# Planner with measured durations and a measured transfer rate, in the two mixed stretches of a long-convolution and MLP kernel

## The chip, the cores and the metric

The kernel runs on one core of one Trainium2 chip. The metric is the device time of one execution in microseconds; of several runs the median counts. One execution of the kernel was also recorded by the hardware profiler, and all rows below come from that one.

## What is computed

Two batches of 12480 positions with 128 channels. A filter is made from position embeddings by a small MLP and an exponential window, the product x * v is convolved with it along the sequence (by FFT in the reference), the result is multiplied by x, and every position then goes through a leaky MLP of width 2048.

```python
h_mlp = np.maximum(pos_emb @ w1, 0.0) @ w2
h_filt = h_mlp * np.exp(-0.01 * pos)[:, None]
u = x * v
Uf, Hf = np.fft.rfft(u, n=2 * S, axis=1), np.fft.rfft(h_filt, n=2 * S, axis=0)
y = np.fft.irfft(Uf * Hf[None], n=2 * S, axis=1)[:, :S, :]
attn = x * y
h = attn.reshape(B * S, D) @ w_in
out = (np.maximum(h, 0.0) + alpha * np.minimum(h, 0.0)) @ w_out
```

## The kernel before

The FFT is done as matmuls, on values split into two float16 halves (a high part and the remainder). The 128 channels come in two groups. For each group the kernel takes chunks of four channels through a first transform over time (stage 1), then runs a loop over pairs of frequencies that multiplies with the filter (stage 2), then transforms back (stage 3) and stores to g_d in HBM. Behind that comes the MLP (phase B), which holds most of the span and is not touched.

Stage 1 of one pair of chunks is, per chunk: a load of x and of v (lines 696, 697), the product P = x * v (line 700), its square on ACT (703); per pair the norm by PE (711) and the sum and the scale of the pair on DVE (717, 332 to 334, the last writes s_u); per chunk again the scaling S (728), the high half on ACT (734), the remainder L (737), twelve matmuls on PE (771 to 773), and the split of their result into z by ACT (783) and DVE (786). P, S and L may run on DVE or on POOL. There are 16 pairs in each group.

The first mixed stretch interleaves stage 1 of the first group with the making of the filter: sixteen hidden-layer products (load 401, PE 406, DVE 409, ACT 413), their sum (DVE 426, "gather"), the scales, eight parts (ACT 451, DVE 452), the w2p halves (444, 445) and the filter's final products (PE 467 to 469, ACT 488, DVE 492). The second mixed stretch lies between the two frequency loops. It interleaves the end of the first loop, stage 3 of the first group (PE 986 to 988, ACT 998 and 1000, DVE 1003, store 1019) and stage 1 of the second group, whose filter chunks are loaded again (758). The loads of the next loop's tables (817) close it.

In both, the order on each engine's queue comes from a planner, the class Plan. Each operation is entered with an engine, a duration in ns, what it reads and writes, and buffers it needs from small pools (in the second stretch: three PSUM tiles "mm", seven x, three v, three uhl, two gst). Plan.run then lists operations: it takes the engine on which something can start first, lets all that could start there within `patience` ns of it compete, and takes the one with the smallest start plus `urge` times its due place. The due place is a + b * i for the i-th step of its kind, from `pace` (h: hidden layer in the first stretch, filter chunks in the second; w: rest of the filter; u, v: pairs of chunks; s: stage 3). An operation that may go to DVE or POOL takes the engine on which it would end first, with `bias` ns added to DVE. Only the resulting order, engine and buffer are used: at run time each engine works through its queue in that order, and waits by semaphores.

```python
near = [c for c in could[best[1]] if c[0] <= best[0][0] + self.patience]
t, _, k = min(near, key=lambda c: c[0] + self.urge * c[1])
```

All loads and stores go out through the SP queue in the planned order, so an issue that waits for a buffer holds those behind it. The rows name the tiles "ring" and "first" (the buffers of both pools), "mm" and "mb" (PSUM), "z" and "s_u".

## Time and profile before

| | us |
|---|---|
| median of three timed runs | 1669.67 |
| lowest and highest of them | 1668.25, 1672.24 |
| the profiled execution | 1673.31 |
| its span | 1671.4 |
| DVE, ACT, POOL busy in the span | 1305.9, 1335.6, 1055.1 |
| PE busy (modelled ends) | 1565.8 |

The mixed stretches can be told from the timeline of DVE: the first runs from the start to about 149 us, the first frequency loop to about 264, the second mixed stretch to about 393, and the second loop starts at 399. In a group of instructions, "x27 | 36.2, 1346 | 13.5" means 27 instructions, 36.2 us busy, 1346 ns each on average, and 13.5 us in which the engine sat idle just before one of them; what ended the idle time follows. A wait "A <- B" says that A, first in its queue, waited for B.

### The profile page before, as it was taken

The page shows a single profiled execution, that of the slowest core. Times are in us where ns is not written, and L with a number is a line of the kernel's source. Part 1 is how long each engine was busy: PE and PEld are TensorE (multiplying, and loading weights), DVE is VectorE, ACT ScalarE, POOL GpSimd, SP SyncE. Part 2 cuts the span into 40 slices and gives each one's busy share as a digit, 9 for nine tenths or more (in the row PEclk, how much of TensorE's full clock was granted, in tenths as well). Part 3 has the DMA queues.
Part 4 walks back from the last instruction along what each step waited for, and adds up shares of the span by engine and source line. Part 5 has one row for each costly group of instructions (what it writes and reads, how often), then busy time and mean ns, then how long its engine had stood idle before and what let it go on. Part 6 is the DMA issues. An engine that isn't in the chain of part 4 may idle for free.

```text
span 1671.4 us, 34331 instructions
## 1 busy us (share of the span) xinstructions
PE 1565.8 (94%) x13452; PEld 1105.8 (66%) x13452; DVE 1305.9 (78%) x1892; ACT 1335.6 (80%) x2211; POOL 1055.1 (63%) x742
## 2 busy tenths in 40 slices
PE   6878887998998699999999999999999999999998
PEld 4778777888998456666666666566666666666664
DVE  7888999887998577777777777777777777777775
ACT  5776776776876588888888888888888888888886
POOL 6586887886987455665556655565556655565554
PEclk8897998999999899999999999999999999999999
DMA  7443345874447902022020220212202112022000
GB/s 207 123 134 131 112 136 167 241 231 142 135 135 207 232 26 56 20 74 56 20 56 20 75 55 20 56 35 59 55 21 55 54 41 56 20 63 62 25 11 20
DMA packets 95567, 143.95 MB, mean 86 GB/s; under 512 B 7121, under 2 KB 64179, under 8 KB 93965
## 3 DMA queue, kind: packets, MB, share of 16 engines
q1 hardware_dynamic: 94285, 141.06, 29.6%
q8 instruction: 105, 1.72, 0.5%
q10 hardware_dynamic: 1120, 0.70, 0.1%
q14 instruction: 57, 0.47, 0.1%
HBM read 100.06 MB, written 41.68 MB: 85 GB/s over the span
## 4 chain that ended last, share of the span: by engine, by line
PE 74%; DVE 10%; POOL 4%; issue 4%; DMA 4%; ACT 3%; SPq 0%; POOLq 0%; ACTq 0%; DVEq 0%
PE hp L1244 30%; PE o L1244 30%; DVE ring L885 4%; DMA first<-in_xv 2%; POOL ring L737 2%; DVE ring L895 2%; PE yp L279 1%; PE yp L280 1%; PE yp L281 1%; PE mm L986 1%; PE mm L988 1%; PE mm L987 1%; POOL ring L700 1%; DVE z L786 1%; POOL ring L728 1%
## 5 line engine op out<-in xcount | busy, mean ns | idle before, releaser
L1244 PEld LDWEIGHTS <-w 128*128 128x128 f16 x6144 | 591.7, 97 | 431.6 <-issue 15.2
L1331 POOL TENSOR_TENSOR g_lo<-ring,g_hi 128x780 f16<-128x780 f32 x288 | 479.7, 1670 | 483.4 <-ACT g_hi L1330 483.4
L1324 DVE SCALAR_TENSOR_TENSOR ring<-ring,keep,hp 128x780 f32<-128x780 f32 x512 | 524.8, 1025 | 270.5 <-ACT ring L1323 261.4
L1323 ACT ACTIVATE ring<-hp 128x780 f32<-128x780 f32 x512 | 419.1, 818 | 162.3 <-PE hp L1244 161.4
L1244 PE MATMUL hp<-ah,w 128*128 128x390 f16 x2048 | 506.3, 328 | 3.7 <-DVE ring L1324 2.7
L1244 PE MATMUL o<-g_hi,w 128*128 128x390 f16 x2048 | 504.3, 328 | 0.9 <-ACT ot L1345 0.7
L1330 ACT ACTIVATE g_hi<-ring 128x780 f16<-128x780 f32 x512 | 433.5, 847 | 0.4 <-DVE ring L1324 0.3
L1244 PE MATMUL hp<-alo,w 128*128 128x390 f16 x1024 | 253.3, 328 | 0.8 <-DVE alo L1236 0.8
L1244 PE MATMUL o<-g_lo,w 128*128 128x390 f16 x1024 | 252.7, 328 | 0.6 <-POOL g_lo L1331 0.6
L1331 DVE TENSOR_TENSOR g_lo<-ring,g_hi 128x780 f16<-128x780 f32 x224 | 229.1, 1023 | 0.0
L1206 POOL TENSOR_TENSOR gl<-gt,gh 90x1024 f16<-90x1024 f32 x62 | 154.5, 2491 | 1.5 <-ACT gh L1205 1.5
L885 DVE TENSOR_TENSOR ring<-mm,ring 128x512 f32<-128x512 f32 (+2 forms) x188 | 116.2, 658 | 11.3 <-ACT ring L873 8.7
L986 PE MATMUL mm<-t,z 128*128 128x128 f16 x512 | 104.5, 235 | 10.5 <-DVE ring L1003 5.6
L912 POOL TENSOR_TENSOR z<-ring,z 128x512 f16<-128x512 f32 x88 | 105.0, 1194 | 6.8 <-ACT z L908 6.8
L987 PE MATMUL mm<-t,z 128*128 128x128 f16 x512 | 103.7, 234 | 0.0
L988 PE MATMUL mm<-t,z 128*128 128x128 f16 x512 | 103.6, 234 | 0.0
L771 PE MATMUL mm<-t,ring 98*128 98x180 f16 x320 | 83.5, 264 | 18.7 <-DVE z L786 5.2
L890 POOL TENSOR_TENSOR ring<-ring 128x256 f32<-128x256 f32 (+1 forms) x90 | 81.2, 902 | 30.7 <-DVE ring L885 22.2
L783 ACT ACTIVATE z<-mm 128x720 f16<-128x720 f32 (+1 forms) x99 | 73.9, 759 | 32.0 <-PE mm L773 31.6
L786 DVE TENSOR_TENSOR z<-mm,z 128x720 f16<-128x720 f32 (+1 forms) x99 | 85.2, 876 | 17.5 <-ACT z L783 16.8
L1003 DVE TENSOR_TENSOR ring<-mm,ring 90x504 f32<-90x504 f32 (+2 forms) x132 | 80.4, 655 | 13.9 <-ACT ring L1000 12.6
L773 PE MATMUL mm<-t,ring 98*128 98x180 f16 x320 | 83.6, 264 | 7.4 <-POOL ring L737 7.3
(195 smaller groups left out, 2955.3 us busy)
## 6 DMA issues: line engine op xcount, KB each, us to landing
g_d<-ring SPq DMA_DIRECT2D x32, 720.0 KB
gt<-g_d SPq DMA_DIRECT2D x16, 1440.0 KB
ring<-in_tw SPq DMA_DIRECT2D x34, 512.0 KB
ring<-in_xv SPq DMA_DIRECT2D x72, 196.0 KB
xt<-in_xt SPq DMA_DIRECT2D x31, 390.0 KB
out_t<-ot SPq DMA_DIRECT2D x31, 390.0 KB
first<-in_xv SPq DMA_DIRECT2D x56, 196.0 KB
first<-in_tw SPq DMA_DIRECT2D x12, 512.0 KB
```

Source lines behind the costliest of these rows:

```text
L786: ve.tensor_tensor(out=zb[:, 1, :, x:y, cs], in0=pv()[:, :, x:y], in1=zb[:, 0, :, x:y, cs], op=ALU.subtract)
L885: ve.tensor_tensor(out=t[:, :, m], in0=p[:, :, m], in1=hs[:, a:a + 1, m].to_broadcast([128, 2, (b1 - b0) * 2 * ZC]), op=ALU.mult)
L912: e.tensor_tensor(out=zl, in0=v, in1=zh, op=ALU.subtract)
L986: te.matmul(o, hi, t3[:, 0], start=True, stop=False)
L987: te.matmul(o, hi, t3[:, 1], start=False, stop=False)
L988: te.matmul(o, lo, t3[:, 0], start=False, stop=True)
L1206: po.tensor_tensor(out=dl, in0=src, in1=dh, op=ALU.subtract)
L1244: te.matmul(o[:, b, :TOK], w, d[:, b], start=start and n == 0, stop=stop and n == 2)
L1323: ac.activation(neg, h, AF.Relu, scale=-1.0)
L1324: ve.scalar_tensor_tensor(out=acts[n], in0=neg, scalar=keep[:, f:f + 1], in1=h, op0=ALU.mult, op1=ALU.add)
L1330: ac.activation(gh, a, AF.Copy)
L1331: (po if n % 2 or n % NFT == 0 else ve).tensor_tensor(out=gl, in0=a, in1=gh, op=ALU.subtract)
```

## The change

Only the planner's numbers change. The constructor gets a factor `flow`, 1 by default, that multiplies the duration of every DMA entry; both mixed stretches set it to 360 / 255, so a transfer is planned at 255 bytes per ns instead of 360. Durations of P, S and L and of the filter's part are replaced. The due places, `urge`, `patience` and `bias` of both stretches are replaced. The last plan, before phase B, keeps its numbers.

```diff
+        self.guard, self.bias, self.warm, self.flow = {}, 0, 0, 1
...
     def op(self, engine, ns, fn, r=(), w=(), rows=128):
         k = len(self.ops)
+        ns = ns * self.flow if engine == "DMA" else ns
...
-            P.op("DVE", dve_ns(2 * w), lambda: ve.scalar_tensor_tensor(out=lo, in0=src, scalar=sr, in1=hi, op0=ALU.mult, op1=ALU.subtract),
+            P.op("DVE", 1080, lambda: ve.scalar_tensor_tensor(out=lo, in0=src, scalar=sr, in1=hi, op0=ALU.mult, op1=ALU.subtract),
...
-                    P.op({"DVE": dve_ns(512), "POOL": 1225}, 0, product, r=[v[j]], w=[x[j]])
+                    P.op({"DVE": 880, "POOL": 1320}, 0, product, r=[v[j]], w=[x[j]])
...
-                    P.op({"DVE": 600, "POOL": 1001}, 0, scaled, r=[("s", g, n)], w=[x[j]])
+                    P.op({"DVE": 1150, "POOL": 1060}, 0, scaled, r=[("s", g, n)], w=[x[j]])
...
-                    P.op({"DVE": 600, "POOL": 1113}, 0, low, r=[x[j]], w=[h])
+                    P.op({"DVE": 1000, "POOL": 1260}, 0, low, r=[x[j]], w=[h])
...
+            P.flow = 360 / 255
...
-            P.pace.update(h=(0, 692), w=(18681, 2576), u=(10132, 13596), v=(98023, 3578))
-            P.urge, P.patience, P.bias = .5, 100, 1112
+            P.pace.update(h=(-48954, 2278), w=(20007, 3535), u=(21788, 17237), v=(94626, 3276))
+            P.urge, P.patience, P.bias = 3.7, 44, 1354
...
+            P.flow = 360 / 255
...
-            P.pace.update(h=(-9e3, 100), s=(0, 3600), u=(20394, 3768))
-            P.urge, P.patience, P.bias = 3, 50, 1377
+            P.pace.update(h=(-30228, 41505), s=(-14272, 7297), u=(23122, 6183))
+            P.urge, P.patience, P.bias = 3.1, 0, 911
```

The changed file has one more line from line 143 on, two more from 1051 and three more from 1070, so line 409 of before is 410 of after, 700 is 701, 1003 is 1004 and 1019 is 1020.

Near the start of the first stretch, on DVE, before: hidden rows (409) mixed with the first pair's sum and scale (717, 332 to 334) and a product (700).

```order
L409 SCALAR_TENSOR_TENSOR z<-mm_95,ring 128x336
L717 TENSOR_REDUCE mb_97<-mb_97 128x8
L332 TENSOR_SCALAR mb_97<-mb_97 128x8
L333 TENSOR_SCALAR mb_97<-mb_97 128x8
L334 TENSOR_SCALAR s_u<-mb_97 128x8
L409 SCALAR_TENSOR_TENSOR z<-mm_96,ring 128x336
L409 SCALAR_TENSOR_TENSOR z<-mm_94,ring 128x336
L700 TENSOR_TENSOR ring<-ring,first 98x512
L409 SCALAR_TENSOR_TENSOR z<-mm_95,ring 128x336
L409 SCALAR_TENSOR_TENSOR z<-mm_96,ring 128x336
L409 SCALAR_TENSOR_TENSOR z<-mm_94,ring 128x336
L700 TENSOR_TENSOR ring<-ring,first 98x512
```

The same place in the changed kernel, where the first pair's scale follows the last hidden row and stands right ahead of the gather (427):

```order
L410 SCALAR_TENSOR_TENSOR z<-mm_94,ring 128x336
L410 SCALAR_TENSOR_TENSOR z<-mm_95,ring 128x336
L410 SCALAR_TENSOR_TENSOR z<-mm_96,ring 128x336
L410 SCALAR_TENSOR_TENSOR z<-mm_94,ring 128x336
L718 TENSOR_REDUCE mb_97<-mb_97 128x8
L333 TENSOR_SCALAR mb_97<-mb_97 128x8
L334 TENSOR_SCALAR mb_97<-mb_97 128x8
L335 TENSOR_SCALAR s_u<-mb_97 128x8
L427 TENSOR_REDUCE n_113<-nq 128x1
L428 TENSOR_SCALAR nb<-ones,n_113 128x128
L333 TENSOR_SCALAR mb_98<-n_113 128x1
```

All sixteen hidden rows now stand ahead of any work on x and v. The second pair's sum and scale stood ahead of the gather too (rows 717, 332 to 334 again, a few rows on); in the changed kernel they stand behind seven of the eight parts (453) and twelve filter halves (493).

Near the start of the second stretch, on DVE, before: pairs of stage-3 rows (1003) ahead of the first scale, which row 334 writes.

```order
L700 TENSOR_TENSOR ring<-ring,first 98x512
L912 TENSOR_TENSOR z<-ring,z 128x2x3x64
L1003 TENSOR_TENSOR ring<-mm_96,ring 90x2x63x4 x2
L1003 TENSOR_TENSOR ring<-mm_94,ring 90x2x63x4 x2
L1003 TENSOR_TENSOR ring<-mm_95,ring 90x2x63x4 x2
L717 TENSOR_REDUCE mb_97<-mb_97 128x8
L1003 TENSOR_TENSOR ring<-mm_96,ring 90x2x63x4 x2
L786 TENSOR_TENSOR z<-mm_94,z 128x180x4
L332 TENSOR_SCALAR mb_97<-mb_97 128x8
L333 TENSOR_SCALAR mb_97<-mb_97 128x8
L334 TENSOR_SCALAR s_u<-mb_97 128x8
```

The same place in the changed kernel, where four rows less of stage 3 (1004, "x2" counts two) stand ahead of that scale and an S (729) follows it at once:

```order
L913 TENSOR_TENSOR z<-ring,z 128x2x3x64
L1004 TENSOR_TENSOR ring<-mm_96,ring 90x2x63x4 x2
L1004 TENSOR_TENSOR ring<-mm_94,ring 90x2x63x4 x2
L1004 TENSOR_TENSOR ring<-mm_95,ring 90x2x63x4 x2
L787 TENSOR_TENSOR z<-mm_96,z 128x180x4
L718 TENSOR_REDUCE mb_97<-mb_97 128x8
L333 TENSOR_SCALAR mb_97<-mb_97 128x8
L334 TENSOR_SCALAR mb_97<-mb_97 128x8
L335 TENSOR_SCALAR s_u<-mb_97 128x8
L729 TENSOR_TENSOR ring<-ring,s_u 98x512
```

With those just ahead of the pieces (four before, two after), twelve rows of stage 3 precede the first scale before, and eight now. Before, a run of four S rows (728) on DVE comes a little later; the changed kernel has none.

At the end of the second stretch, on SP, before: the last store of stage 3 (1019), then three filter chunks (758) and the next loop's tables (817).

```order
L696 DMA ring<-in_xv 98x512
L697 DMA first<-in_xv 98x512
L758 DMA ring<-h_d 98x1024
L1019 DMA g_d<-ring 90x16x128
L758 DMA ring<-h_d 98x1024 x3
L817 DMA first<-in_tw 128x2048
L817 DMA ring<-in_tw 128x2048 x3
```

The same place in the changed kernel:

```order
L1020 DMA g_d<-ring 90x16x128
L759 DMA ring<-h_d 98x1024
L1020 DMA g_d<-ring 90x16x128
L759 DMA ring<-h_d 98x1024
L818 DMA first<-in_tw 128x2048
L818 DMA ring<-in_tw 128x2048
L1020 DMA g_d<-ring 90x16x128
L818 DMA ring<-in_tw 128x2048 x2
```

The last stores now alternate with the filter chunks, and the very last one stands behind two table loads.

Counted over each stretch, the engines of P, S and L move as follows.

| | DVE before: P, S, L | DVE after | POOL before | POOL after |
|---|---|---|---|---|
| first stretch | 8, 9, 2 | 13, 4, 1 | 24, 23, 30 | 19, 28, 31 |
| second stretch | 5, 9, 0 | 11, 5, 1 | 27, 23, 32 | 21, 27, 31 |

## Rows read from the trace of the kernel before

**Rows 1.** Busy time by stretch; the first row names the columns:

```profile
core 0: us, PE busy (x) PEld busy (x) DVE busy (x) ACT busy (x) POOL busy (x), PEclk, DMA share, GB/s
0.00:149.00 149.00, 110.96 (x1315) 98.50 (x1316) 118.50 (x198) 102.64 (x184) 100.95 (x85) 0.85 0.51 152
264.00:393.20 129.20, 112.04 (x1444) 106.07 (x1443) 108.87 (x197) 90.68 (x210) 102.20 (x86) 0.92 0.72 209
344.00:393.20 49.20, 43.38 (x518) 40.72 (x517) 39.03 (x70) 36.61 (x78) 42.27 (x37) 0.90 0.67 197
```

**Rows 2.** Instruction groups, 0 to 152 us: count, busy, mean, idle:

```profile
L786 DVE TENSOR_TENSOR z<-mm,z 128x720 f16<-128x720 f32 x47 | 41.1, 898 | 8.8 <-ACT z L783 8.4
L737 POOL TENSOR_TENSOR ring<-ring 98x512 f16<-98x512 f32 x30 | 38.2, 1287 | 13.7 <-ACT ring L734 13.6
...
L700 POOL TENSOR_TENSOR ring<-ring,first 98x512 f32<-98x512 f32 x20 | 27.4, 1377 | 17.9 <-DMA first<-in_xv 16.5 <-PE mm L773 1.3
L728 POOL TENSOR_TENSOR ring<-ring,s_u 98x512 f32<-98x512 f32 x23 | 25.4, 1120 | 7.8 <-DVE s_u L334 4.0 <-DVE mb L332 3.8
...
L492 DVE TENSOR_TENSOR z<-mm,z 84x512 f16<-84x512 f32 x16 | 10.1, 676 | 0.8 <-ACT z L488 0.7
...
L452 DVE SCALAR_TENSOR_TENSOR z<-z,sr 128x672 f16<-128x672 f32 x8 | 9.2, 1171 | 0.0
...
L445 DVE SCALAR_TENSOR_TENSOR w2p<-w2b,w2p 128x256 f16<-128x256 f32 x4 | 3.6, 947 | 0.0
```

**Rows 3.** Timeline of DVE, 0 to 60 us: start, length, instruction:

```profile
7.34 0.51 DVE L409 SCALAR_TENSOR_TENSOR z<-mm,ring 128x336 f32<-128x336 f32 x1 [1.31 <-PE mm L406]
8.46 0.51 DVE L409 SCALAR_TENSOR_TENSOR z<-mm,ring 128x336 f32<-128x336 f32 x1 [0.61 <-PE mm L406]
...
26.75 0.17 DVE L334 TENSOR_SCALAR s_u<-mb 128x8 int32<-128x8 int32 x1
...
29.93 0.17 DVE L426 TENSOR_REDUCE n<-nq 128x1 f32<-128x16 f32 x1 [0.64 <-ACT mm L413]
```

**Rows 4.** Timeline of POOL, 0 to 152 us, two rows:

```profile
51.37 3.38 POOL L737 TENSOR_TENSOR ring<-ring 98x512 f16<-98x512 f32 x2 [10.16 <-ACT ring L734]
...
144.06 1.15 POOL L737 TENSOR_TENSOR ring<-ring 98x512 f16<-98x512 f32 x1 [0.25 <-ACT ring L734]
```

**Rows 5.** Instruction groups, 255 to 398 us:

```profile
L737 POOL TENSOR_TENSOR ring<-ring 98x512 f16<-98x512 f32 x32 | 41.4, 1306 | 2.1 <-ACT ring L734 2.1
...
L1003 DVE TENSOR_TENSOR ring<-mm,ring 90x504 f32<-90x504 f32 x64 | 40.4, 671 | 9.0 <-ACT ring L1000 8.4
...
L700 POOL TENSOR_TENSOR ring<-ring,first 98x512 f32<-98x512 f32 x27 | 36.2, 1346 | 13.5 <-DMA first<-in_xv 13.1
...
L728 POOL TENSOR_TENSOR ring<-ring,s_u 98x512 f32<-98x512 f32 x23 | 24.1, 1061 | 8.4 <-DVE s_u L334 8.4
...
L728 DVE TENSOR_TENSOR ring<-ring,s_u 98x512 f32<-98x512 f32 x9 | 11.0, 1249 | 0.0
...
L700 DVE TENSOR_TENSOR ring<-ring,first 98x512 f32<-98x512 f32 x5 | 4.9, 976 | 1.0 <-DMA first<-in_xv 1.0
```

**Rows 6.** Timeline of POOL, 252 to 320 us, two rows:

```profile
284.95 2.04 POOL L728 TENSOR_TENSOR ring<-ring,s_u 98x512 f32<-98x512 f32 x2 [6.55 <-DVE s_u L334]
286.94 5.87 POOL L737 TENSOR_TENSOR ring<-ring 98x512 f16<-98x512 f32 x4
```

**Rows 7.** Line 728, 255 to 400 us: min/median/max ns:

```profile
L728 DVE TENSOR_TENSOR ring<-ring,s_u x9: 678/1336/1667, 287.3 to 379.5; 98x512 f32<-98x512 f32 x9
```

**Rows 8.** Waits, 255 to 395 us: total us, times, longest us:

```profile
POOL ring L700 <- DMA first<-in_xv: 13.1, 9, 2.3
...
SPq L696 <- POOL ring L737: 35.0, 19, 5.3
```

**Rows 9.** Chain of waits, 255 to 400 us: shares by line, and one piece:

```profile
by line: POOL ring L737 16.4%; DMA first<-in_xv 15.0%; issue 14.1%; POOL ring L728 7.0%; POOL ring L700 5.4%; DVE ring L1003 3.3%; DVE ring L728 3.3%; DVE ring L885 3.2%; DMA g_d<-ring 3.1%; DVE z L786 3.1%; DVE ring L895 3.0%; PE mm L773 2
...
275.78 4.55 DMA g_d<-ring
```

More of the change, by code (lines that the diff above doesn't have):

```diff
@@ L135, in __init__ @@
         self.size, self.fifo, self.loose = dict(pools), {p: [] for p in pools}, set()
-        self.guard, self.bias, self.warm = {}, 0, 0
+        self.guard, self.bias, self.warm, self.flow = {}, 0, 0, 1
     def buf(self, pool):
```

## Prediction

> **What bounds the kernel now.** I read first the busy time by stretch. The change reorders two stretches only: from the start to 149 us, and from 264 to 393 us; behind the second, every engine's rows stand as before, apart from line numbers. In neither stretch is one engine full: in the first DVE works 118.5 of 149 us and POOL 101.0; in the second PE 112.0 of 129.2 (modelled ends), DVE 108.9, POOL 102.2 [rows 1]. So what counts is how order and waits couple them.
>
> Next the chain of waits of the second stretch. Lines 737, 728 and 700 on POOL hold 28.8% of it and the loads of v ("first<-in_xv") 15.0%; the largest DVE line has 3.3% [rows 9]. It is a ring: the loader waits for POOL's line 737 to give an x buffer back (35.0 us, 19 times), POOL's line 700 waits for the load (13.1 us, 9 times) [rows 8]. Over the last 49.2 us POOL is busy for 42.3 [rows 1].
>
> In the first stretch, read the timelines. DVE reaches the filter's sum (line 426, "gather") at 29.93 us, and has written the second pair's scale at 26.75 + 0.17 = 26.9 [rows 3]. POOL then sits for 10.16 us before its line 737 at 51.37, because ACT's order holds that row's input behind filter work, and runs its last line 737 until 144.06 + 1.15 = 145.2 [rows 4].
>
> **The change part by part.** Four edits give the planner longer DVE prices, slower transfers, new urgencies and new limits. No instruction's work changes; engine and place do. I write P, S and L for line 700's product, 728's scaling and 737's subtraction (701, 729, 738 after).
>
> *Second stretch, engine choice.* Counted in the order, POOL had 27 P, 23 S, 32 L and gets 21, 27, 31. At 1.346, 1.061 and 1.306 us [rows 5] that is 36.3 + 24.4 + 41.8 = 102.5 before and 28.3 + 28.6 + 40.5 = 97.4 after: about -5.1 by means, -4.3 against the 101.7 that the three groups really add to. I take -4.3. DVE had 5 P, 9 S and gets 11 P, 5 S, 1 L: 6 x 0.976 - 4 x 1.249 [rows 5] + one L, for which I take POOL's 1.306, is +2.2 us, inside the 129.2 - 108.9 = 20.3 us that DVE idles [rows 1]. But the two engines slow each other: four L on POOL took 5.87 us [rows 6], 1.47 each, where one alone took 1.15 [rows 4], while DVE ran S rows. That is +0.3 us on POOL per such DVE row, and there are 3 more: +0.9. Net -3.4. It lies on the path, since POOL and its loads lead the chain.
>
> The same S takes DVE from 678 to 1667 ns [rows 7]. The Trainium skill (SBUF — State Buffer, "Who interferes with whom") says why: a DVE instruction with two SBUF inputs and a GpSimd one that reads SBUF shut each other out for the whole instruction. By that rule each of the 3 added DVE rows would cost POOL a full 0.68 us, 2.0 in all, and the net would be -2.3 instead of -3.4. The mean of the four L, +0.3, speaks for less.
>
> *Second stretch, start.* POOL idles 6.55 us up to 284.95 for the first scale [rows 6]. Ahead of that scale DVE now has 8 rows of line 1003 (1004 after) instead of 12: 4 x 0.671 = 2.7 us sooner [rows 5]. POOL and its loads are 44% of the chain [rows 9], so I book half, -1.4; bounds 0 and -2.7.
>
> *Second stretch, end.* Stage 3 now lasts to the end: 5 z rows instead of 12 follow its last pair on DVE. POOL's last S S L L stays last, so this is booked at 0. The last g_d store goes out behind two table loads, and the next loop's second product waits for it. A store takes 4.55 us [rows 9], with four z pieces and the unscale rows ahead of that product as cover. If the loads are late, it costs up to 4.5; if the evened-out tail shortens PE's queue, up to -3.
>
> *First stretch.* DVE now takes all 16 hidden rows (410) before any work on u. In before, two P, two z rows, one S and two scales stood between them. Hidden rows come every 1.12 us at best (7.34 to 8.46, the second and third); before, the sixteen and the gather took from 7.34 to 29.93, 1.5 us each [rows 3]. With 14 more from 7.34, at 1.12 or at 1.5 us and 0.51 for the last, they end at 23.5 or 28.9; I take the gather at 26.5, 3.4 sooner. The price is at the second pair's scale. Between gather and it stand now 7 parts (1.171), 12 halves of the filter (0.676), 4 w2p rows (0.947) and 2 z rows (0.898) [rows 2]: 8.2 + 8.1 + 3.8 + 1.8 = 21.9 us, and about 4 us of small rows, an estimate (a dozen at 0.17 [rows 3], and the norms of w2b). So it comes at 26.5 + 26 = 52.5, say 53 us, where it was 26.9.
>
> POOL's three groups sum to the same 97.5 us in both orders (24 P, 23 S, 30 L before; 19, 28, 31 after, at 1.377, 1.120, 1.287 [rows 2]). By 53 us it can have done 10 P, 2 S, 2 L, 18.6 us; 78.9 are left, so it ends at 132 plus its idle time. Before, at 51.37, it had done 10 P, 4 S, 4 L, 23.4 us; 74.1 were left and took until 145.2, with 19.7 idle. Break-even is 145.2 - 132 = 13.3 us of idle. With 19.7 the stretch is +6.4 longer; with half, 10, it is -3. I take 13, a change of 0: six P now stand in a row on POOL while it waits, so five pairs lie ready for the scales, and much of the old idle time followed from x buffers held through the 10.16 us. DVE's count barely moves (8 P, 9 S, 2 L to 13, 4, 1), 5 x 0.976 - 5 x 1.249 and one L less, some 2.7 us less by the prices above. Range -6 (7 us of idle) to +9 (rival A).
>
> **Sum.** -3.4 - 1.4 + 0 + 0 = -4.8 us. The profiled execution took 1673.3 us (span 1671.4), so it would give 1668.5. That execution is 3.6 us above the median of the three timed runs, 1669.67, so I predict 1669.67 - 4.8 = 1664.9.
>
> **The rivals.** A difference of 0.2%, 3.3 us, is about what a measurement of this kernel can tell from no change; below 1666.3 is faster, above 1673.0 slower.
>
> *A, POOL's backlog in the first stretch decides (slower).* If hidden rows still come every 1.5 us, the gather falls near 29.5, the second scale near 55.5, and POOL with the old 19.7 us of idle ends at 55.5 + 78.9 + 19.7 = 154.1, +8.9. With -4.8 from the second stretch: 1673.8. It decides once POOL's last L there ends later than 153.3 (+8.1 - 4.8 = +3.3). For it: 19.7 idle us was normal. Against: half of that was waiting for loads and for ACT.
>
> *B, the ring of x buffers holds the second stretch (same).* POOL's saved time turns into waiting for loads, since seven x buffers and a load remain in the ring; only the earlier start counts, -1.4: 1668.3. For it: 13.1 us of load waits already [rows 8]; DMA is 72% busy [rows 1]. Against: over the last 49 us POOL is busier than the transfers (86% to 67% [rows 1]).
>
> *C, the new prices fix the coupling in both stretches (much faster).* POOL idles only 7 us after the second scale, -6, and the second stretch gives its bounds, -4.3 - 2.7 = -7.0: 1656.7. For it: the old plan priced S at 600 ns on DVE, and its mean was 1249 [rows 5]. Against: a mean of 678 to 1667 is not a duration.
>
> *D, the change does not do what it says:* the prices hold only for the old overlap and are wrong again in the new order. Then nothing systematic is left, and it lands with B.
>
> **How the numbers follow.** Forecast 0.37, C 0.17, B with D 0.24, A 0.22. The forecast's own range is 1660 to 1666.3, so faster is 0.37 + 0.17 = 0.54, same 0.24, slower 0.22. For the range I add the ends of the first stretch to the bounds of the second: -6 - 7 = -13, and a little for a shorter tail, gives 1655; +9 with -4.8, and part of the store's 4.5, gives 1677. About one case in ten lies beyond each end: 1655 to 1677.
>
> **What would show it.** In the profile after: the gather by 27 us, and the second scale near 53; POOL's last L of the first stretch at 142 to 148; no wait as long as 10 us on POOL before line 738; the first S of the second stretch some 3 us sooner after its first P; POOL's three groups there near 98 us in sum; the span from the second stretch's first P to its last L shorter by about 5 us. I am wrong if the first stretch ends after 153 us, if POOL's load waits in the second rise from 13.1 by what its work falls, or if the loop behind it opens with DVE waiting for a store.

## The result, and the profile after

The changed kernel takes 1654.61 us (median of 4 runs, 1650.64 to 1657.97), the kernel before 1668.96 us (4 runs beside them): a ratio of 0.9911, with a 95% interval of 0.9883 to 0.9938. That is 14.4 us less, where 4.8 were forecast; the time lies just below the low end of the range, 1655. The two profiled executions stand further apart: 1673.31 us before and 1655.36 after (spans 1671.4 and 1653.6).

The two traces give the gain to the two mixed stretches, in nearly equal halves. Below, the first product of loop 1 (line 886; 885 before) marks the end of the first stretch, and the same line's first row in loop 2 marks the end of the second, which starts with its first P on POOL. P, S and L are the product, the scaling and the subtraction as in the prediction.

| | before | after | |
|---|---|---|---|
| first stretch, from the start | 151.9 us | 143.4 | -8.5 |
| loop 1, to the first P | 112.4 | 112.7 | +0.3 |
| second stretch, first P to loop 2 | 134.7 | 126.9 | -7.8 |
| from there to the end | 1272.4 | 1270.6 | -1.8 |

Both stretches gained more than the range had allowed them (6 and 7 us). One trace tells a stretch's time only to about 3 us: the first two experiments below have stretches in which DVE, ACT and POOL run the same rows in the same order as here, and there the order of the kernel before took 153.4 us in the first stretch (151.9 here), and that of the changed kernel 124.0 in the second (126.9 here). Smaller differences between two traces are not read as differences.

**First stretch.** DVE's timeline after (columns: start, us, engine, line, operation, tiles, count, idle time before and its releaser): the second and the last of the sixteen hidden rows, and the gather, at 29.93 before [rows 3]; then two pieces of POOL's, the first S of the second pair, and POOL's last L (144.06 before [rows 4]).

```profile
7.16 0.51 DVE L410 SCALAR_TENSOR_TENSOR z<-mm,ring 128x336 f32<-128x336 f32 x1 [1.13 <-PE mm L407]
...
21.09 0.51 DVE L410 SCALAR_TENSOR_TENSOR z<-mm,ring 128x336 f32<-128x336 f32 x1 [0.88 <-PE mm L407]
...
22.37 0.16 DVE L427 TENSOR_REDUCE n<-nq 128x1 f32<-128x16 f32 x1
...
51.41 2.64 POOL L729 TENSOR_TENSOR ring<-ring,s_u 98x512 f32<-98x512 f32 x2 [11.26 <-DVE s_u L335]
...
137.12 1.16 POOL L738 TENSOR_TENSOR ring<-ring 98x512 f16<-98x512 f32 x1 [1.51 <-ACT ring L735]
```

POOL waits 11.26 us for the second pair's scale, as was foreseen (it comes at 51.4; the prediction said 53). But then it runs almost through: 86.9 us from there to the end of its last L, against 93.8 before. The windows view of those stretches, before and then after (columns: busy time and count of PE, weight loads, DVE, ACT and POOL, then granted clock, DMA share, GB/s):

```profile
51.40:145.20 93.80, 73.02 (x1025) 70.41 (x1022) 76.89 (x127) 68.20 (x108) 71.91 (x59) 0.84 0.48 144
51.40:138.30 86.90, 70.73 (x984) 66.22 (x981) 76.43 (x131) 68.47 (x110) 78.16 (x64) 0.90 0.54 165
```

78.16 of 86.9 us busy leaves 8.7 idle, where it was 21.9 before (the prediction's 19.7 counts the work by means, 74.1 us, where 71.9 were run). What POOL waited for from 51.5 us on (columns: line waited for, us, times, longest), after, then before; the longest one of each is the wait that ends at 51.4:

```profile
POOL ring L729 <- DVE s_u L335: 13.8, 4, 11.3
POOL ring L738 <- ACT ring L735: 4.2, 3, 1.7
POOL ring L701 <- DMA ring<-in_xv: 1.0, 2, 0.7
POOL ring L701 <- DMA first<-in_xv: 0.7, 2, 0.4
```

```profile
POOL ring L737 <- ACT ring L734: 12.8, 3, 10.2
POOL ring L700 <- DMA first<-in_xv: 6.7, 5, 3.1
POOL ring L728 <- DVE mb L332: 3.8, 1, 3.8
POOL ring L700 <- issue: 3.1, 1, 3.1
POOL ring L728 <- DVE s_u L334: 3.0, 3, 2.4
POOL ring L700 <- PE mm L773: 1.3, 1, 1.3
POOL ring L700 <- DMA ring<-in_xv: 1.1, 1, 1.1
```

Waits for x and v behind the scale fell from 7.8 us (6.7 + 1.1) to 1.7. That is 6.1 of the 13.2 us of idle time that went; waits for scales, without the one that ends at 51.4, gave another 4.3 (6.8 to 2.5), and the other waits the rest. Ahead of the scale the load waits stayed: over the whole stretch POOL waits 14.6 us for v, against 16.5 before.

**Second stretch.** The windows view, cut at the first S (first P to first S, then first S to the last L), before and then after:

```profile
264.30:284.90 20.60, 16.16 (x218) 15.66 (x216) 17.89 (x31) 12.29 (x36) 9.25 (x9) 0.83 0.61 174
284.90:392.70 107.80, 95.11 (x1218) 89.64 (x1218) 90.68 (x166) 77.89 (x174) 92.44 (x76) 0.94 0.74 215
```

```profile
256.10:270.90 14.80, 12.56 (x164) 12.37 (x165) 13.28 (x25) 8.74 (x26) 8.46 (x8) 0.77 0.44 132
270.90:372.70 101.80, 91.76 (x1246) 87.36 (x1245) 92.73 (x171) 80.56 (x180) 89.38 (x74) 0.98 0.78 225
```

The end of the stretch after, in the timelines of POOL (its last two L) and DVE:

```profile
370.38 2.32 POOL L738 TENSOR_TENSOR ring<-ring 98x512 f16<-98x512 f32 x2
...
374.82 1.27 DVE L1004 TENSOR_TENSOR ring<-mm,ring 90x504 f32<-90x504 f32 x2 [0.41 <-ACT ring L1001]
...
378.23 0.97 DVE L787 TENSOR_TENSOR z<-mm,z 128x64 f16<-128x64 f32 x2 [0.45 <-ACT z L784]
...
382.97 1.29 DVE L886 TENSOR_TENSOR ring<-mm,ring 128x512 f32<-128x512 f32 x2 [1.20 <-ACT ring L874]
```

So the 7.8 us are made of four pieces: the first S comes 5.8 us sooner after the first P (20.6 to 14.8); from there to the last L POOL works 3.1 us less (92.4 to 89.4) and idles 3.0 us less (15.4 to 12.4); and 4.0 us are given back behind the last L, since loop 2 now starts 10.3 us after it (372.7 to 383.0), where it was 6.3: DVE still has stage-3 rows and z rows until 379.2. POOL's three groups and its waits for loads, to be held against [rows 5] and [rows 8]:

```profile
L738 POOL TENSOR_TENSOR ring<-ring 98x512 f16<-98x512 f32 x31 | 38.6, 1260 | 4.8 <-ACT ring L735 4.8
L729 POOL TENSOR_TENSOR ring<-ring,s_u 98x512 f32<-98x512 f32 x27 | 31.7, 1190 | 8.3 <-DVE s_u L335 8.3
L701 POOL TENSOR_TENSOR ring<-ring,first 98x512 f32<-98x512 f32 x21 | 27.2, 1305 | 3.4 <-DVE ring L1004 2.1 <-DMA first<-in_xv 1.4
L701 DVE TENSOR_TENSOR ring<-ring,first 98x512 f32<-98x512 f32 x11 | 13.2, 1210 | 2.4 <-POOL ring L738 2.4
L729 DVE TENSOR_TENSOR ring<-ring,s_u 98x512 f32<-98x512 f32 x5 | 4.1, 829 | 0.1
```

### The profile page after: what moved, and what is told of

It is laid out like the page before. It is cut to its first block, busy times and chain, and to the rows that moved or that the text cites. A ratio compares the mean times of both kernels' runs of the same rounds, so it can differ in the third digit from the quotient of the medians.

```text
span 1653.6 us, 34337 instructions
## 1 busy us (share of the span) xinstructions
PE 1558.2 (94%) x13452; PEld 1097.7 (66%) x13452; DVE 1305.6 (79%) x1894; ACT 1335.1 (81%) x2211; POOL 1052.9 (64%) x740
## 4 chain that ended last, share of the span: by engine, by line
PE 76%; DVE 9%; POOL 5%; DMA 4%; issue 3%; ACT 3%; SPq 1%; POOLq 0%; ACTq 0%; DVEq 0%
PE o L1247 31%; PE hp L1247 31%; DVE ring L886 4%; DVE ring L896 2%; POOL ring L738 2%; DMA first<-in_xv 1%; PE yp L280 1%; PE yp L281 1%; PE yp L282 1%; PE mm L987 1%; POOL ring L729 1%; PE mm L989 1%; PE mm L988 1%; PE mm L861 1%; PE mm L859 1%
## 5 line engine op out<-in xcount | busy, mean ns | idle before, releaser
L886 DVE TENSOR_TENSOR ring<-mm,ring 128x512 f32<-128x512 f32 (+2 forms) x188 | 116.2, 658 | 12.1 <-ACT ring L874 11.3
L987 PE MATMUL mm<-t,z 128*128 128x128 f16 x512 | 104.2, 234 | 14.6 <-ACT z L909 7.3
L891 POOL TENSOR_TENSOR ring<-ring 128x256 f32<-128x256 f32 (+1 forms) x90 | 81.3, 903 | 32.6 <-DVE ring L886 26.5
L787 DVE TENSOR_TENSOR z<-mm,z 128x720 f16<-128x720 f32 (+1 forms) x99 | 85.3, 875 | 5.7 <-ACT z L784 5.4
L772 PE MATMUL mm<-t,ring 98*128 98x180 f16 x320 | 80.2, 254 | 10.0 <-DVE ring L493 3.1
L987 PEld LDWEIGHTS <-z 128*128 128x128 f16 x512 | 77.5, 151 | 17.0 <-DVE ring L1004 9.1
L1004 DVE TENSOR_TENSOR ring<-mm,ring 90x504 f32<-90x504 f32 (+2 forms) x132 | 80.2, 655 | 10.7 <-ACT ring L1001 10.2
```

The source lines that it names most:

```text
L787: ve.tensor_tensor(out=zb[:, 1, :, x:y, cs], in0=pv()[:, :, x:y], in1=zb[:, 0, :, x:y, cs], op=ALU.subtract)
L886: ve.tensor_tensor(out=t[:, :, m], in0=p[:, :, m], in1=hs[:, a:a + 1, m].to_broadcast([128, 2, (b1 - b0) * 2 * ZC]), op=ALU.mult)
L987: te.matmul(o, hi, t3[:, 0], start=True, stop=False)
```

## The experiments

Two questions stood open: which part of the change pays, and why both stretches gained some 8 us where 0 and 4.8 were forecast. Stretch times are read from one trace of each run as in the table above; ratios come from the timed runs and are to the kernel before on the same chip, with 95% intervals.

**One stretch alone.** The new numbers for the first stretch only (e1), for the second only (e2):

```diff
-P.op({"DVE": 880, "POOL": 1320}, 0, product, ...)
+P.op({"DVE": dve_ns(512) if shared else 880, "POOL": 1225 if shared else 1320}, 0, product, ...)
...
-P.flow = 360 / 255                              (second plan; its pace, urge, bias as before)
+P.flow = 1
```

> New prices, rate and urgencies in the first mixed stretch alone; the second is planned as before. Theory T (each stretch gains by itself): the first product of loop 1 comes at 143.4 +-1 us (as in the changed kernel; 151.9 before) and the second stretch takes 134.6 +-1.5 us from the first P to the first product of loop 2 (as before), so 8.5 us less in all, ratio 0.995. Rival R (the second stretch's gain is carried over from the first, by where buffers or stores stand when it starts): the second stretch shortens here too, 12 us or more less in all, ratio 0.993 or less.

> The second mixed stretch alone is planned anew; the first as before. Theory T: loop 1 starts at 151.9 +-1 us, the second stretch takes 126.8 +-1.5 us, 7.8 us less in all, ratio 0.995. Rival R: the second stretch stays within 2 us of 134.6 and the ratio is 0.999 to 1.000.

e1: loop 1 at 143.9 us, second stretch 135.0, ratio 0.9974 (0.9959 to 0.9989). e2: loop 1 at 153.4, second stretch 124.0, ratio 0.9950 (0.9931 to 0.9969). Each stretch gains by itself, and the stretch that was left as it was gains nothing from the other; the rival falls. Two times lie outside of theory T's bounds, 153.4 (151.9 +-1) and 124.0 (126.8 +-1.5), though the order is the same. By the timed runs the first stretch's numbers are worth 0.26% and the second's 0.50%, so that the two halves need not be equal.

**Which numbers.** The change has three parts: prices (P, S, L and the filter's part), the transfer rate, and the urgencies (pace, urge, patience, bias). Six more kernels make the eight combinations complete. The edits, each one or two of these three:

```diff
-P.flow = 360 / 255                                         (rate)
+P.flow = 1
...
-P.op({"DVE": 1150, "POOL": 1060}, 0, scaled, ...)          (prices)
+P.op({"DVE": 600, "POOL": 1001}, 0, scaled, ...)
...
-P.urge, P.patience, P.bias = 3.1, 0, 911                   (urgencies)
+P.urge, P.patience, P.bias = 3, 50, 1377
```

> All new durations and the new rate, but pace, urge, patience and bias of before in both stretches. Theory E (my forecast's: what counts is which engine takes P, S and L): the second stretch has the same engine split as the changed kernel (P 21, S 27, L 31 on POOL), so it keeps at least 3.4 us of its gain; first stretch within 1 us of 151.9. Rival O (the order counts: when the first gathers, scales and loads come): without the new urgencies nearly all of the gain is gone, 0 to 3 us less than before in all, with the first scale of the second stretch (first S) about 20 us after the first P as before, and the second scale of the first stretch at 53 us or later. The kernel's own planner, with the durations that were measured, says the same as O: its planned ends are 133.9 and 132.5 us here, against 122.5 and 119.8 us for the changed kernel.

> The new pace, urge, patience and bias in both stretches, with the old prices and the old rate. Rival O (order alone): nearly all of the 14 us comes, ratio 0.991 to 0.993. Theory J (durations and urgencies only work together; urgencies found for one set of durations are worse than the old ones with another): under half comes, 0 to 6 us less, and the first stretch is no shorter than before (loop 1 starts at 151 us or later), since with too cheap transfers POOL is again given products of which the x and v have not landed. Theory E (engine split alone) gives 0 +-2, since the old prices give POOL P 24, S 24 and L 31 of 32 in the first stretch (before: 24, 23, 30; changed: 19, 28, 31).

> The changed kernel with the old transfer rate in both plans (the new prices and urgencies stay). Theory W (POOL waits for landings that the old rate promised too early): POOL's waits for x and v come back (15 us or more in the first stretch, 8 us or more in the second against 1.4), the first stretch ends at 150 us or later, the second takes 132 us or more: 10 to 14 us longer than the changed kernel. Rival N (the rate hardly matters, since the order of the loads is set by the urgencies): within 3 us of the changed kernel.

> The changed kernel with the old prices of P, S, L and of the filter's part (the new rate and urgencies stay). Theory W: the rate is what the urgencies needed, so most of the gain stays: loop 1 at 143 to 147 us, the second stretch 127 to 130 us. Rival N (the prices carry the gain): loop 1 at 150 us or later, the second stretch 132 us or longer, with P on DVE seldomer than in the changed kernel (11 P on DVE there in the second stretch).

> The kernel before with the new transfer rate alone in both plans. Theory W: POOL's waits for x and v in the second stretch fall from 13.1 to under 7 us, and both stretches gain 2 us or more, though the urgencies are the old ones. Rival J (only all three together pay): no stretch gains over 1.5 us, one of them loses.

> The kernel before with the new prices alone. Theory W and rival J both expect no gain: the first stretch 0 to 6 us longer, the second 0 to 5 us longer, POOL's waits for x and v at 8 us or more in the second. Theory E (the split is what pays): the second stretch 131 us, -3.4.

The last two columns are POOL's waits for x and v: in the first stretch behind 51.5 us, and in the second from the first P to the last L.

| new in it | run | first stretch | second | ratio | waits 1st | waits 2nd |
|---|---|---|---|---|---|---|
| nothing | before | 151.9 | 134.7 | 1 | 7.8 | 13.1 |
| rate | e14 | 146.5 | 137.6 | 1.0014 (0.9997 to 1.0031) | 3.2 | 9.8 |
| prices | e15 | 159.7 | 144.6 | 1.0085 (1.0054 to 1.0116) | 10.2 | 17.5 |
| urgencies | e4 | 151.9 | 130.0 | 0.9983 (0.9970 to 0.9996) | 14.5 | 16.7 |
| rate, prices | e3 | 154.3 | 141.6 | 1.0075 (1.0052 to 1.0098) | 7.6 | 11.3 |
| rate, urgencies | e8 | 163.4 | 134.4 | 1.0059 (1.0034 to 1.0084) | 5.7 | 7.7 |
| prices, urgencies | e5 | 160.2 | 140.2 | 1.0040 (1.0022 to 1.0058) | 8.1 | 19.4 |
| all | after | 143.4 | 126.9 | 0.9911 (0.9883 to 0.9938) | 1.7 | 1.4 |

Read the parts alone: only the rate helps the first stretch (-5.4), only the urgencies help the second (-4.7), and the prices by themselves cost both (+7.8 and +9.9). Of the pairs none is faster than before in the first stretch, and in the second the best is even with it. Only all three give both gains. (The traced execution of e5 is the slowest of its eight, 10.2 us above their median, so its two stretch times are upper ends; its ratio, from all eight, still says slower than before.) In each pair of rows that differ by the rate alone, POOL's load waits are shorter with it, in both stretches; the same order can differ by 3 us in this too (e1, whose second stretch is planned as before, has 9.5 us of them there).

The expectations fared as follows. The engine split does not carry the gain (theory E): e3 and e5 have the changed kernel's counts in the second stretch (21, 27 and 31 on POOL) and take 141.6 and 140.2 us. e3, for which theory O expected 0 to 3 us less than before, is slower by 0.75%. In e4 theory O falls and J holds. In e5 theory W holds, with a loss larger than its 10 to 14 us; in e8 it falls: with the rate and the urgencies but the old prices both gains are gone. In e14 both sides fall: the first stretch gains, the second does not, and its load waits are not under 7 us. e15 costs more than either side had allowed.

What the rate alone does to the first stretch shows in POOL's timeline of e14: it waits 5.93 us for a scale, until 42.76, and has its next L at 45.37, where POOL of the kernel before sat until 51.37 after 10.16 us without work [rows 4].

```profile
42.76 2.65 POOL L729 TENSOR_TENSOR ring<-ring,s_u 98x512 f32<-98x512 f32 x2 [5.93 <-DVE s_u L335]
45.37 1.77 POOL L738 TENSOR_TENSOR ring<-ring 98x512 f16<-98x512 f32 x1
```

But fewer waits are not yet time: e8 waits 5.4 us less than before in the second stretch and is no faster, e4 waits 3.6 us longer and is 4.7 faster. Nor is an early first S. Here is the second stretch of all eight, cut at the first S, at the end of POOL's last L, and at loop 2 (us; e2 has the order of the changed kernel there):

| run | first P to first S | POOL works, up to its last L | POOL idles meanwhile | last L to loop 2 | second stretch |
|---|---|---|---|---|---|
| before | 20.6 | 92.4 | 15.4 | 6.3 | 134.7 |
| e14, rate | 15.6 | 86.8 | 27.4 | 7.8 | 137.6 |
| e15, prices | 19.8 | 89.3 | 27.5 | 8.0 | 144.6 |
| e4, urgencies | 11.4 | 87.1 | 22.3 | 9.3 | 130.0 |
| e3, rate and prices | 20.3 | 91.0 | 22.6 | 7.8 | 141.6 |
| e8, rate and urgencies | 14.5 | 85.3 | 17.0 | 17.6 | 134.4 |
| e5, prices and urgencies | 12.5 | 88.3 | 30.0 | 9.5 | 140.2 |
| after, all | 14.8 | 89.4 | 12.4 | 10.3 | 126.9 |
| e2, all | 14.6 | 90.0 | 10.5 | 8.9 | 124.0 |

The first S comes as early as in the changed kernel, or earlier, in e4, e5 and e8, and nearly so in e14, and POOL has less work behind it in all of them. What sets the changed kernel apart is that POOL does not idle longer for it: in the others 1.6 to 14.6 us more than before, or, in e8, a long end, take the early start back in part or whole. The granted clock of TensorE does not set it apart. Behind the first S its mean rose from 0.94 of full speed to 0.98, but it was 0.98 in e4 too, where that part took 109.4 us, no less than the 107.8 before (windows rows of e4, cut at the first S):

```profile
265.00:276.40 11.40, 8.11 (x107) 7.91 (x108) 10.49 (x19) 6.40 (x19) 8.87 (x8) 0.72 0.38 126
276.40:385.80 109.40, 96.26 (x1298) 90.48 (x1297) 95.97 (x178) 81.41 (x186) 87.06 (x72) 0.98 0.75 214
```

**The engine split alone.** Each P, S and L is bound to the engine of the other kernel, and the plan's other numbers stay:

```diff
-P.op({"DVE": 880, "POOL": 1320}, 0, product, ...)
+P.op(only(0, shared, n + j, {"DVE": 880, "POOL": 1320}), 0, product, ...)
...
+def only(kind, shared, n, prices):
+    e = "DVE" if SPLIT[shared][kind][n] == "D" else "POOL"
+    return {x: c + 1e6 * (x != e) for x, c in prices.items()}
```

> The changed kernel, but each P, S and L of both stretches is bound to the engine that it had before (POOL: P 24, S 23, L 30 in the first stretch; 27, 23, 32 in the second), planned with the new prices, rate and urgencies. Theory E (the engine choice is worth 3.4 us in the second stretch and nothing in the first, as the prediction has it): the second stretch takes 130 +-1.5 us, loop 1 starts at 143 to 145 us. Rival J (order, engines and urgencies are one plan, and another split breaks it): both stretches lose 5 us or more, the second takes 132 us or more, loop 1 starts at 148 us or later.

> The kernel before, with each P, S and L bound to the engine that it has in the changed kernel (19, 28, 31 and 21, 27, 31 on POOL); old prices, rate and urgencies. Theory E: the second stretch gains 3.4 us, 131.3 +-1.5 us instead of 134.7; the first stays within 1.5 us of 151.9. Rival J: nothing is gained, both stretches within 2 us of before or longer, POOL's waits for loads in the second stretch still 8 us or more.

e10, the kernel before with the new split: 152.7 and 133.8 us, ratio 1.0023 (1.0005 to 1.0040). e9, the changed kernel with the old split: 161.0 and 141.7 us, ratio 1.0111 (1.0079 to 1.0142). In e10 POOL's work from the first P to the last L does fall, by 5.6 us (101.69 before), and here is the windows row, and behind it what POOL waits for:

```profile
265.00:392.50 127.50, 108.91 (x1435) 103.11 (x1434) 108.08 (x198) 90.82 (x210) 96.12 (x82) 0.95 0.72 210
```

```profile
POOL ring L729 <- DVE s_u L335: 15.7, 6, 9.0
POOL ring L701 <- DMA first<-in_xv: 9.5, 5, 3.5
POOL ring L738 <- ACT ring L735: 3.6, 4, 1.5
```

POOL waits 15.7 us for scales where it waited 8.4: the freed time turned into a wait for DVE's scale rows, which the old order brings no sooner. Theory E falls: the stretch is 0.9 us shorter, which one trace can't tell from nothing, and the timed runs are slower than before where 3.4 us would be a ratio of 0.998. Rival J holds for both kernels.

**The loads.** First v was left out altogether, with P squaring x (e6, e7):

```diff
-sy.dma_start(out=vr(j), in_=A["xv"][g, n + j, :, 1, :])
...
-either[e].tensor_tensor(out=xr(j), in0=xr(j), in1=vr(j), op=ALU.mult)
+either[e].tensor_tensor(out=xr(j), in0=xr(j), in1=xr(j), op=ALU.mult)
```

> The changed kernel without the loads of v: P squares x instead of multiplying by v, the plan is untouched. Half of the load traffic of both stretches is left out. Theory W: POOL's waits for x are nearly gone at once, little is gained, 0 to 4 us in each stretch. Rival X (the DMA rate bounds even the new plan): 6 us or more in a stretch.

> The kernel before without the loads of v, in the same way. Theory W (late landings cost the old plan its time): it gains most of what the change gains, 6 to 9 us in each stretch, and stands within 3 us of the changed kernel without these loads. Rival O (the order itself costs: which chunk's scale and P come when): it gains under 3 us in each stretch and the two kernels without loads of v stand 9 us or more apart. In the first stretch the trace speaks for O (POOL waits for loads 14.6 us in the changed kernel, 16.5 before), in the second for W (1.4 against 13.1).

The kernel before gained 10.0 and 9.3 us (141.9 and 125.4; ratio 0.9888, 0.9859 to 0.9917), the changed one 4.6 and 3.4 (138.8 and 123.5; ratio 0.9834, 0.9805 to 0.9862). That looks like theory W, but these runs changed a second thing: P on POOL got cheaper. Its rows of the second stretch in e7, and then before (columns: shortest, median, longest ns, first and last start):

```profile
L701 POOL TENSOR_TENSOR ring<-ring x27: 1033/1047/1493, 254.3 to 359.8; 98x512 f32<-98x512 f32 x27
```

```profile
L700 POOL TENSOR_TENSOR ring<-ring,first x27: 1258/1299/1759, 264.3 to 377.9; 98x512 f32<-98x512 f32 x27
```

A quarter of a microsecond on 27 rows is 6.8 us of POOL's work. So the loads were taken away again with P as it is: v is loaded only the first time that each of its buffers is used in a stretch.

```diff
-sy.dma_start(out=vr(j), in_=A["xv"][g, n + j, :, 1, :])
+if not (g, v[j].pool, v[j].i) in once: once.add(...), sy.dma_start(out=vr(j), ...)
```

> The changed kernel with v loaded only once for each buffer in a stretch (5 loads of v in the first stretch, 3 in the second, instead of 32); P multiplies by what stands in the buffer, so P keeps its instruction and its price, unlike in e6 where P read one tile and got 0.2 us cheaper on POOL. Left out: 27 and 29 loads of v. Theory W (late landings are what the change removes): 0 to 2 us less in each stretch. Rival X (half of what e6 gained came from loads): 2 to 4 us less in each stretch.

> The kernel before with v loaded only once for each buffer in a stretch. Theory W: each stretch gains 5 us or more (loop 1 at 147 us or sooner, the second stretch 129.5 us or less), and stands within 4 us of the changed kernel with few v. Rival O (the gain of e7 came from the cheaper P on POOL, 24 x 0.23 = 5.5 and 27 x 0.25 = 6.8 us): under 4 us in each stretch, and the kernels stay 5 us or more apart in each.

The kernel before gained 5.0 us in the first stretch and 3.7 in the second (146.9 and 131.0; ratio 0.9960, 0.9929 to 0.9991), the changed one 1.2 and 3.6 (142.2 and 123.3; ratio 0.9883, 0.9855 to 0.9912). With few loads the two kernels are 4.7 us apart in the first stretch, where they were 8.5, and 7.7 in the second, where they were 7.8. So theory W holds for about half of the first stretch's gain and for 0 to 3 us of the second's: there e2, with all loads, was at 124.0 us already, and by that the two orders are 10.7 apart with all loads and 7.7 with few. The timed runs say the same of the whole: with few loads the kernels are 12.1 us apart (1662.64 and 1650.57), with all of them 14.4. In the second stretch the chain of waits had misled: the share of the loads of v in it fell from 16.1% to 6.7% (the head of the chain's shares over the second stretch, before and after). 16.1% of 134.7 us are 21.7, and yet leaving out 29 of these 32 loads was worth 3.7 us to the kernel before.

```profile
by line: POOL ring L737 17.7%; DMA first<-in_xv 16.1%; issue 14.4%; POOL ring L728 7.5%; POOL ring L700 5.8%; DVE ring L1003 3.6%; DVE ring L728 3.5%; DMA g_d<-ring 3.4%; DVE z L786 3.3%; PE mm L773 2.5%; PE mm L771 2.2%; PE mm L772 2.1%; P
```

```profile
by line: issue 11.0%; POOL ring L738 10.0%; PE mm L987 7.0%; PE mm L989 6.7%; DMA first<-in_xv 6.7%; POOL ring L729 6.6%; PE mm L988 6.4%; DVE ring L1004 4.8%; PE mm L772 4.6%; PE mm L773 4.3%; PE mm L774 4.2%; DMA ring<-h_d 3.9%; POOL ring
```

The kernel before without these loads shows why: from the first P to the last L its load waits fell from 13.1 to 5.2 us, but the first S still came 20.4 us after the first P, and about half of these 7.9 us went into other waits of POOL, which idles 22.6 us in all there and 26.7 before (the windows row up to the first S; POOL's waits in the whole stretch):

```profile
259.20:279.60 20.40, 16.48 (x217) 15.91 (x215) 17.61 (x30) 12.35 (x36) 10.37 (x9) 0.83 0.48 134
```

```profile
POOL ring L729 <- DVE s_u L335: 9.1, 2, 7.1
POOL ring L701 <- DMA ring<-in_xv: 5.2, 4, 1.7
POOL ring L738 <- ACT ring L735: 3.9, 3, 2.8
```

**Truer prices still.** The trace after shows many rows longer than the planner's prices. Most were set as measured there (not S on DVE in the second stretch, which got 1000 ns where the trace has 829), with urgencies searched anew:

```diff
-P.op("ACT", act_ns(512), square, ...)
+P.op("ACT", 630, square, ...)
...
-{"DVE": 1150, "POOL": 1060}
+{"DVE": 1000 if shared else 1170, "POOL": 1190 if shared else 1157}
...
-P.urge, P.patience, P.bias = 3.1, 0, 911
+P.urge, P.patience, P.bias = 1e6, 3, 931
```

> The changed kernel, with the other durations of both stretches set to what the changed kernel's trace shows as well (z rows 897 and 771 ns where the planner had 817 and 651, squares and highs 630 instead of 520, the filter's parts 1308, stage 3's rows 670 and 937, P on DVE 1055 and 1210), and urgencies searched anew for these. The planner's own ends: 132.5 and 128.3 us, where the changed kernel's urgencies would give 145.9 and 137.0 with these durations. Theory M (truer durations with urgencies to match go on paying): 3 to 8 us less than the changed kernel in each stretch, loop 1 at 135 to 140 us, the second stretch 119 to 124 us. Rival D (durations are measured in one overlap and don't hold in another order): within 3 us of the changed kernel in each stretch, or slower.

Loop 1 at 150.8 us, the second stretch 126.4; 1661.22 us, ratio 0.9943 (0.9922 to 0.9964). The second stretch is even with the changed kernel, the first 7.4 us slower. Theory M falls. The waits for x and v behind 51.5 us are 7.2 us again, though the plan has the new rate. In this one plan truer prices were worth nothing, so the truth of the prices does not explain the change.

## Why the prediction was right or wrong

**The sign and the engine work were right.** POOL's three groups of the second stretch went from 101.7 us busy to 97.5 (38.6 + 31.7 + 27.2), 4.2 less, where -3.4 was booked. The prediction's 97.4 only looks like this number: it is count times mean, which counts the small overlaps of successive rows twice, and taken so the rows now give 98.6, against 102.5 before. The charge for mutual slowing, +0.9, did come, but not where the means show it: S on POOL went from 1061 ns [rows 5] to 1190, L from 1306 to 1260. Here are S and L on POOL in the second stretch, before and after (shortest, median and longest ns):

```profile
L728 POOL TENSOR_TENSOR ring<-ring,s_u x23: 1032/1041/1502, 284.9 to 388.9; 98x512 f32<-98x512 f32 x23
L737 POOL TENSOR_TENSOR ring<-ring x32: 1146/1186/1921, 286.9 to 391.5; 98x512 f16<-98x512 f32 x32
```

```profile
L729 POOL TENSOR_TENSOR ring<-ring,s_u x27: 1031/1040/1991, 270.9 to 369.4; 98x512 f32<-98x512 f32 x27
L738 POOL TENSOR_TENSOR ring<-ring x31: 1151/1179/1634, 273.7 to 371.5; 98x512 f16<-98x512 f32 x31
```

The medians of S are the same. POOL's rows come in two lengths, S near 1.04 or 1.49 us, L near 1.17 or 1.62, P near 1.28 or 1.73 (and in each kernel one that is longer still, 1.92 and 1.99). There were 13 long ones before (1 S, 9 L, 3 P) and 15 after (8 S, 6 L, 1 P), and a P, S or L of DVE ran beside each of them. Taken over the median of the short rows, that is 6.3 us of POOL's time before and 7.3 after, an estimate. The Trainium skill (SBUF — State Buffer, "Who interferes with whom") would have charged more than the prediction, 2.0 us for the 3 DVE rows more, by the prediction's estimate. The trace agrees that the two engines hold each other up, at about 0.45 us for a row of POOL that is hit.

**The step that failed in the second stretch is the pricing of the start, and of POOL's waits behind it.** The start was priced by four rows of line 1004 on DVE, 2.7 us, and halved to -1.4. The first S came 5.8 us sooner and, with the urgencies alone (e4), 9.2 sooner. The bound of -2.7 was no bound: it counted one engine's rows ahead of the scale, while the first pair's norm, too, began 8.7 us after the first P instead of 13.6. The end, booked at 0, gave 4.0 us back: not by the store that was feared (loop 2 opens with 1.20 us behind ACT), but by z rows and stage 3 behind the last L. POOL's idle time behind the first S, for which there was no term, fell by 3.0 more. Of -5.8 - 3.1 - 3.0 + 4.0 only the second was in the sum at its size. And "it lies on the path, since POOL and its loads lead the chain" does not hold of the work by itself: e10 has the work's gain and not the time. Nor does an early start count by itself, as e5, e8 and e14 show; in the changed kernel it shows in full, and POOL's idle time did not rise for it.

**In the first stretch the failed step is the idle time behind the scale.** It was taken at 13 us, a 10 was named and not taken, and 8.7 came, near rival C's 7. The scale came at 51.3 us, near the 53 foreseen, by luck in part: the sixteen hidden rows came every 1.0 us (7.16 to 21.09), faster than the 1.12 that was called the best, and the gather at 22.4 instead of 26.5, but from there to the scale it took 28.9 us where 26 were counted. The 78.9 us of work behind it were right (78.2). Against the booked end of 144.9 (53 + 78.9 + 13) POOL's last L ended at 138.3, outside of the 142 to 148 that were to be the sign: 4.3 us for the idle time, 1.6 for the scale, 0.7 for the work. Loop 1 then started 5.1 us behind it instead of 6.7, another 1.6, and with the 0.3 from break-even that is the 8.5. The working put the idle time down to x buffers held behind the 10.16 us wait. But e13 keeps that wait (10.4 us) and still gains 5.0 with most loads of v gone, and e14, told only the rate, gains 5.4. So what was left out is an edit of its own: the new transfer rate stood in the list of edits and had no term anywhere. It is worth 5.4 us to the first stretch by itself, and by its ratio the changed kernel without it (e5) loses all that it had gained, and more.

**The rivals.** C came near the time with 1656.7, for a wrong reason: "the new prices fix the coupling". The prices alone are the worst of the parts (e15), though without them the other two pay nothing (e8), and they don't hold even where they are used: S on DVE is priced at 1150 ns and took 829 in the second stretch, P at 880 and took 1210. D, which said that, expected nothing to be left; it was right on the prices and wrong on the time. B held that POOL's saved time would turn into load waits: where the old order stayed (e10) it turned into scale waits instead, and in the changed kernel into neither. A's 19.7 us of idle time did not stay.

**What stays open.** That three sets of numbers which each do little or harm give 16 us of trace together is shown, not explained. The new urgencies give both gains with the new prices and the new rate and with no other pair that was run; which rows of the order that follows make POOL idle less, no run shows. The 4.7 us of the first stretch and the 7.7 of the second that stay with few loads are put down to that order for want of another difference: the two kernels run the same instructions and differ only in their order, engine and buffers, and the engines by themselves were worth nothing (e10).

## What to carry to other kernels

Where a planner's prices and its urgencies change together, an edit is not the sum of its parts: no single part here was worth more than 5.4 us in a stretch, and every pair cost time, so count the order that comes out, not the prices that went in. Ask of each engine's freed work which wait takes its place; the new split freed 5.6 us of POOL and gave nothing that the runs could tell where the order of the scales stayed. And give every edit in the list a term with two bounds, a transfer rate above all: a load's share of the chain of waits says where the chain went, not what the stretch gains when the load is gone. And take the same order's time twice before reading a difference of a few microseconds between two traces.

## What the runs showed of the hardware

P on POOL, 98x512 in f32, took 1258 to 1299 ns (shortest and median) with two different input tiles, and 1033 to 1047 with the same tile twice. It is the operand and not the missing load: with most loads of v gone and two tiles kept (e13) it took 1257 to 1297. On DVE the two forms differ little at their shortest (677 and 679 ns in the same runs; medians 991 and 1040). An experiment that replaces an operand to save a load has thus changed the instruction's price too.

In the second stretch, P, S and L on POOL took about 0.45 us longer, in one step, in 28 of 161 cases (before and after together), each time beside a P, S or L of DVE; 18 others had such a row of DVE beside them and stayed short. Of those beside which DVE ran only rows that read PSUM (tiles mm and mb), 106 were short and none long.
